# Fifteen small loads put ahead of the tail's loads on one issuing queue

## The chip, the core and the metric

The program runs on one core of one Trainium2 chip. The metric is the device time in microseconds (us) of that core. Data comes from the chip's memory through 16 DMA engines; the loads are issued by SyncE (SP), and one load of 128 rows is split over all 16 engines, 8 rows each. The engines that compute are TensorE (PE, with its weight loads as PEld), VectorE (DVE) and ScalarE (ACT); GpSimd (POOL) only builds constants at the start.

## What is computed

One token goes through attention with cached keys and values and then through a gated feed-forward layer, all in 32-bit floats. There are 32 heads with 8192 cached positions and 192 channels each, the model width is 640 and the hidden width 1536.

```
q      = (layernorm(x) @ wq) as 32 heads of 192
scores = q . k_cache * 192**-0.5            # 32 x 8192
o      = softmax(scores) . v_cache          # 32 x 192
h      = x + o @ wo
g, u   = layernorm(h) @ W_gate, layernorm(h) @ W_up
out    = h + (g * (g > 0) * u) @ W_down
```

Keys and values are 403 MB, and everything that is read is 446 MB. Each byte is used once.

## The kernel before, in words

The host lays the inputs out in rows of 128 partitions, one DRAM array for each load, so that a load is 128 long contiguous rows. Three big buffers on chip, slot_x, slot_y and slot_z, each hold up to 65,280 bytes in a partition. The loads go through them in turn: while one buffer is read by TensorE, the others are being filled.

The heads are worked through in this way. Head 0 is the start. Then a loop of 10 turns takes three heads in each turn (units a, b and c). A turn issues five loads: row_1 and row_2 of a turn at the end of the turn before, and row_3, row_4 and row_5 inside it. A unit multiplies the query with the keys (line 180), transposes the scores on DVE (line 385), takes the exponential on ACT (line 482) and multiplies with the values (line 187). The last head, the output projection and the feed-forward layer stand behind the loop, in a tail written out once.

What sets the order is a set of hand-written semaphores. SP waits until a buffer has been used up (free[i], counted by PE or DVE) and until its load before has landed (land[i]), then issues the next load into it. All loads stand in one SP program and are issued in the order of the code (line 533 is the helper that records every load). A load into slot_x in the tail, for example, stands behind a wait on free[4], which DVE gives once unit c of the last turn has used its keys.

Behind the loop's last turn SP issues, in this order: row_t1 into slot_x (keys of the last head and a quarter of the values of the head before), row_t2a and row_t2b into slot_z (values and projection weights), then, when free[5] has come, row_t3 and row_up into slot_y, then, when fin has come, row_gate and four pieces of row_down into slot_x. At the end, when the result stands in the tile o4 (fout), SP and ACT store one half of it each, and SP waits for both stores.

In the tail PE waits for row_t1 before the last head's scores (line 263), for row_t3 before the last values (line 280), for row_up before the up projection (line 300), for row_gate before the gate projection (line 306), and for the four pieces of row_down inside the down projection (lines 318 and 325). DVE multiplies up and gate (line 465) and transposes the product (line 466) between the last two.

Of the kernel before, what the change touches and what calls it, by code (L numbers as in the profile page):

```python
# [85 lines left out]
def build(nc, arrays):  # L86
    dram = {k: nc.dram_tensor(k, v.shape, F32, kind="ExternalInput").ap() for k, v in arrays.items()}
    out = nc.dram_tensor("out", (1, 1, D), F32, kind="ExternalOutput").ap()
    sb = lambda name, shape: nc.alloc_sbuf_tensor(name, list(shape), F32).ap()
# [26 lines left out]
    gu = sb("gu", [P, FG])  # L116
    guT = sb("guT", [P, FJ, 32])
    o4 = sb("o4", [P, DG])

    ps = lambda name, w: nc.alloc_psum_tensor(name, [P, w], F32).ap()  # L120
    sc = ps("sc", 1024)
# [2 lines left out]
    sem = nc.alloc_semaphore  # L124
# [3 lines left out]
    free = [sem(f"free{i}") for i in range(6)]  # L128
    tl = {n: sem(f"tl_{n}") for n in ("t1", "t2a", "t2b", "t3", "up", "gate", "d0", "d1", "d2", "d3")}
    fin, fout, hsem, out_a = (sem(n) for n in ("fin", "fout", "hsem", "out_a"))  # L130
    cst_pe, cst_ve, hdve, hrs, out_s = (sem(n) for n in ("cst_pe", "cst_ve", "hdve", "hrs", "out_s"))

    def wait(eng, s, n, sub=0, **kw):
        w = eng.wait_ge(s, n)  # L134
        if sub:
            w.then_inc(s, -sub)
        return w
# [392 lines left out]
    sp = nc.sync  # L530

    def load(t, src, s):
        sp.dma_start(t, src).then_inc(s, 16)

    def sync_program():
        load(Y[:, 0:W_P], dram["row_p"], land[5])
        r1, r2, r3, r4, r5 = (dram[f"row_{i}"] for i in range(1, 6))
        load(X[:, 0:W_1], r1[0], land[1])
        load(Z[:, 0:W_2], r2[0], land[2])

        def turn(i):
            wait(sp, free[5], 1, 1)
            wait(sp, land[5], 16, 16)
            load(Y[:, 0:W_3], r3[i], land[3])
            wait(sp, free[1], 2, 2)
            wait(sp, land[1], 16, 16)
            load(X[:, 0:W_4], r4[i], land[4])
            wait(sp, free[3], 2, 2)
            wait(sp, land[3], 16, 16)
            load(Y[:, 0:W_5], r5[i], land[5])  # L550
            wait(sp, free[2], 1, 1)
            wait(sp, land[2], 16, 16)
            wait(sp, free[4], 1, 1)
            wait(sp, land[4], 16, 16)

        with sp.Fori(0, NTURN - 1) as i:
            turn(i)
            load(X[:, 0:W_1], r1[i + 1], land[1])
            load(Z[:, 0:W_2], r2[i + 1], land[2])
        turn(NTURN - 1)  # L560
        load(X[:, 0:W_T1], dram["row_t1"], tl["t1"])
        load(Z[:, 0:W_T2A], dram["row_t2a"], tl["t2a"])
        load(Z[:, W_T2A:W_T2A + W_T2B], dram["row_t2b"], tl["t2b"])
        wait(sp, free[5], 1, 1)
        wait(sp, land[5], 16, 16)
        load(Y[:, 0:W_T3], dram["row_t3"], tl["t3"])
        load(Y[:, W_T3:W_T3 + W_UP], dram["row_up"], tl["up"])
        wait(sp, fin, 1, 1)
        load(X[:, 0:W_UP], dram["row_gate"], tl["gate"])
        for n, (a, b) in enumerate(DOWN):  # L570
            load(X[:, W_UP + a:W_UP + b], dram["row_down"][:, a:b], tl[f"d{n}"])
        wait(sp, fout, 1)
        load(out[0, 0, 0:D // 2].rearrange("(g n) -> g n", g=2), o4[31:33, :], out_s)
        wait(sp, out_s, 16, 16)
        wait(sp, out_a, 16, 16)
        wait(sp, fout, 1, 1)

    programs = ((ET.PE, tensor_program), (ET.DVE, vector_program), (ET.Activation, scalar_program),
                (ET.Pool, pool_program), (ET.SP, sync_program))
    for e, _ in programs:  # L580
        nc.br(f"prog_{e.name}", engines=[e])
# [13 lines left out]
```

## Time and profile before

| What | Value |
|---|---|
| median of 3 runs | 1038.7 us (1038.47 to 1038.83) |
| the profiled execution's own time | 1039.63 us |
| span in its profile | 1038.3 us |
| bytes read | 445.94 MB, 429 GB/s over the span |
| packets of the SP queue, share of the 16 DMA engines' time | 99.4% |
| PE busy | 547.4 us (53%) |
| DVE busy | 188.2 us (18%) |
| mean granted TensorE clock | 0.767 |

The span runs from the first to the last instruction that was recorded; 1.3 us of the profiled execution lie outside it. A DMA packet is what one engine moves for one row, and each load ends on each engine with a 4-byte packet that counts up the load's semaphore. In a narrow window the profile puts a packet's whole time at its start, so a DMA share above 1.00 there counts starts and not use. Instructions also come to the chip by DMA, in packets of 16 KB on a queue of their own ("q8 instruction").

### The profile page before, as it was taken

The numbers are of one execution on the slowest core, as the hardware profiler recorded it, in microseconds if no ns is written. First come the engines' busy times: TensorE is split into PE (matmuls) and PEld (weight loads), VectorE is DVE, ScalarE is ACT, GpSimd is POOL, SyncE is SP. The second block draws the span as 40 slices with busy tenths as digits, with TensorE's granted clock in tenths as the row PEclk, the third lists the DMA queues.
The fourth block names the chain that finished last, engine by engine and source line by source line (L and its number), as shares of the span: only waits on it lengthen the run. The fifth ranks groups of instructions, "written<-read, shape, count | busy, mean of one in ns | idle before, by whom it ended". The sixth has DMA issues, their size and how long they took to land. (4 is left out here: it accounts for less than half of the span.)

```text
span 1038.3 us, 10306 instructions
## 1 busy us (share of the span) xinstructions
PE 547.4 (53%) x4492; PEld 176.3 (17%) x4492; DVE 188.2 (18%) x478; ACT 41.2 (4%) x137; POOL 1.2 (0%) x11
## 2 busy tenths in 40 slices
PE   0746446456363563654544546536465463564676
PEld 0211112112121120111111112112111121121123
DVE  1211221112122021221121220212221121220111
ACT  1000000000000000000000000000000000000010
POOL 0000000000000000000000000000000000000000
PEclk9876867768677677776787867867877778687787
DMA  9999999999999999999999999999999999999997
GB/s 402 441 432 425 434 435 431 445 420 435 435 439 433 425 438 436 440 427 432 435 435 426 433 438 431 444 426 433 433 438 438 420 438 436 438 432 425 432 427 326
DMA packets 8800, 446.07 MB, mean 430 GB/s; under 512 B 980, under 2 KB 1112, under 8 KB 1240
## 3 DMA queue, kind: packets, MB, share of 16 engines
q1 hardware_dynamic: 8788, 445.94, 99.4%
q8 instruction: 7, 0.11, 0.0%
q14 instruction: 1, 0.01, 0.0%
q10 hardware_dynamic: 4, 0.00, 0.0%
HBM read 445.94 MB, written 0.00 MB: 429 GB/s over the span
## 5 line engine op out<-in xcount | busy, mean ns | idle before, releaser
L180 PE MATMUL sc<-slot_x,qs 128*32 128x512 f32 x1008 | 150.9, 743 | 109.6 <-DMA slot_x<-row 99.9
L187 PE MATMUL po<-slot_y,p 128*2 128x384 f32 x1152 | 117.9, 562 | 80.2 <-DMA slot_y<-row 77.4
L187 PE MATMUL po<-slot_z,p 128*2 128x384 f32 x560 | 72.5, 671 | 91.7 <-DMA slot_z<-row 88.4
L180 PE MATMUL sc<-slot_y,qs 128*32 128x512 f32 x288 | 54.1, 913 | 83.0 <-DMA slot_y<-row 82.5
L187 PE MATMUL po<-slot_x,p 128*2 128x384 f32 x336 | 43.6, 651 | 86.1 <-DMA slot_x<-row 86.1
L373 DVE COPY oc<-od 128x2 f32<-128x2 f32 x32 | 5.1, 159 | 389.5 <-PE od L206 389.5
L385 DVE STREAM_TRANSPOSE st<-sc 128x512 f32<-128x512 f32 x64 | 45.7, 714 | 164.4 <-PE sc L180 164.4
L180 PEld LDWEIGHTS sc<-slot_x,qs 128*32 128x32 f32 x1008 | 35.4, 134 | 200.8 <-DMA slot_x<-row 106.3
L187 PEld LDWEIGHTS po<-slot_y,p 128*2 128x2 f32 x1152 | 29.1, 94 | 167.7 <-DMA slot_y<-row 86.5
L391 DVE TENSOR_REDUCE m<-pt 128x1 f32<-128x128 f32 x32 | 9.3, 292 | 162.6 <-PE pt L199 162.6
L187 PEld LDWEIGHTS po<-slot_z,p 128*2 128x2 f32 x560 | 15.0, 102 | 138.3 <-DMA slot_z<-row 95.6
L474 ACT COPY qs<-q_ps 128x96 f32<-128x96 f32 x32 | 7.7, 239 | 766.9 <-ACTq L134 766.9
L367 DVE SCALAR_TENSOR_TENSOR prod<-slot_y,xn,prod 128x192 f32<-128x192 f32 x88 | 36.9, 419 | 3.1
L180 PEld LDWEIGHTS sc<-slot_y,qs 128*32 128x32 f32 x288 | 11.4, 154 | 113.8 <-DMA slot_y<-row 83.4
L180 PE MATMUL sc<-slot_z,qs 128*32 128x512 f32 x240 | 27.6, 592 | 0.0
L187 PEld LDWEIGHTS po<-slot_x,p 128*2 128x2 f32 x336 | 8.6, 94 | 109.5 <-DMA slot_x<-row 88.0
L203 PEld LDWEIGHTS od<-mrl,ob 128*128 128x128 f32 x132 | 18.1, 199 | 34.2 <-issue 34.2
L478 ACT COPY ob<-po 128x384 f32<-128x384 f32 x32 | 15.3, 479 | 181.1 <-ACTq L134 181.1
L203 PE MATMUL od<-mrl,ob 128*128 128x1 f32 x132 | 20.8, 262 | 1.6 <-PEq L134 1.6
L194 PE MATMUL q_ps<-pat,prod 128*128 128x96 f32 x64 | 15.4, 323 | 8.5 <-PEq L134 8.5
L365 DVE TENSOR_SCALAR prod<-slot_y,xn 128x192 f32<-128x192 f32 x22 | 6.9, 315 | 65.4 <-DMA slot_y<-row 65.3
L376 DVE SCALAR_TENSOR_TENSOR accs<-slot_y,oc,accs 128x640 f32<-128x640 f32 x21 | 18.5, 879 | 0.0
(95 smaller groups left out, 248.6 us busy)
## 6 DMA issues: line engine op xcount, KB each, us to landing
slot_x<-row SPq DMA_DIRECT2D x10, 8160.0 KB, 26.9
slot_z<-row SPq DMA_DIRECT2D x10, 8160.0 KB, 45.8
slot_y<-row SPq DMA_DIRECT2D x10, 8160.0 KB, 24.7
slot_x<-row SPq DMA_DIRECT2D x10, 7680.0 KB, 35.6
slot_y<-row SPq DMA_DIRECT2D x10, 7584.0 KB, 27.1
slot_x<-row_t SPq DMA_DIRECT2D x1, 7680.0 KB, 25.2
slot_y<-row_p SPq DMA_DIRECT2D x1, 7136.0 KB, 19.6
slot_z<-row_t2a SPq DMA_DIRECT2D x1, 5088.0 KB, 36.9
```

Source lines behind the costliest of these rows:

```text
L180: m = te.matmul(sc[Q(g), half * 512:half * 512 + 512], qs[:, 32 * part:32 * part + 32], blk(half, part * 4 + g), start=(part == 0), stop=( ...
L187: m = te.matmul(po[32 * g:32 * g + 2, 0:PW], p[:, 2 * i:2 * i + 2], blk(i), start=(i < 4), stop=(i >= 28))
L194: te.matmul(q_ps[:, 0:96], prod[:, 0:P], pat[:, 0, :], start=True, stop=False)
L203: te.matmul(od[:, 0:1], ob[:, k * DH:k * DH + P], mrl[:, k:k + 1], start=(k == 0), stop=(k == 1))
L365: dv(ve.tensor_scalar(prod, w3[:, 0, :], xn[:, 0:1], None, op0=ALU.mult), w=first)
L367: dv(STT(prod, w3[:, j, :], xn[:, j:j + 1], prod, op0=ALU.mult, op1=ALU.add), w="self", inc=d2p if j == DJ - 1 else None)
L373: dv(ve.tensor_copy(oc, od[:, 0:2]), w=pd())
L376: dv(STT(accs[:, 0:D], w[:, 0:D], oc[:, 0:1], accs[:, 0:D], op0=ALU.mult, op1=ALU.add), w="self", inc=inc)
L385: return dv(ve.transpose(st[:, s], sc[:, s]), w=w)
L391: dv(ve.reduce_max(vec["m1"], pt[:, 0:P], axis=AX.X, negate=True), w=pd(), inc=d2a)
L474: op(ac.copy(qs, q_ps[:, 0:96]), inc=a2p)
L478: op(ac.copy(ob, po[:, 0:PW]), inc=a2p)
```

## The change

A tile "mark" of 16 partitions and 2048 columns is added behind all other tiles, and a semaphore msem. Behind the loop's last turn and ahead of row_t1, SP issues fifteen loads into it: the first of 15 rows, the next of 14, down to one of 1 row, each row 128 floats (512 bytes) from the start of the first rows of row_up. Each goes to its own columns, nothing reads them, and nothing waits for them but one wait on msem (15 loads of 16 counts each) at the very end, between the wait for ACT's store and the last wait on fout. No other instruction is changed; lines behind the additions are numbered higher by 1, 2 and 4.

```diff
@@ tiles and semaphores
+    mark = sb("mark", [16, 2048])
...
+    msem = sem("msem")
@@ sync_program, behind the loop
         turn(NTURN - 1)
+        for k in range(15, 0, -1):
+            load(mark[0:k, 128 * k:128 * k + 128], dram["row_up"][0:k, 0:128], msem)
         load(X[:, 0:W_T1], dram["row_t1"], tl["t1"])
         load(Z[:, 0:W_T2A], dram["row_t2a"], tl["t2a"])
@@ sync_program, at its end
         wait(sp, out_s, 16, 16)
         wait(sp, out_a, 16, 16)
+        wait(sp, msem, 240, 240)
         wait(sp, fout, 1, 1)
```

On SP, behind the loop, this is the order before. The first row is the loop's last load into slot_y.

```order
L533 DMA slot_y<-row 128x15168
L533 DMA slot_x<-row_t 128x15360
L533 DMA slot_z<-row_t2a 128x10176
L533 DMA slot_z<-row_t2b 128x6144
L533 DMA slot_y<-row_t 128x7104
```

With the change, fifteen small loads stand between the first two of these rows. The last four of them and what follows read so:

```order
L535 DMA mark<-row_up 4x128
L535 DMA mark<-row_up 3x128
L535 DMA mark<-row_up 2x128
L535 DMA mark<-row_up 1x128
L535 DMA slot_x<-row_t 128x15360
L535 DMA slot_z<-row_t2a 128x10176
L535 DMA slot_z<-row_t2b 128x6144
```

The three loads row_t1, row_t2a and row_t2b, which SP issued at once when slot_x was free, are now issued behind fifteen others.

## The prediction, on record before the changed kernel ran

> **What bounds the kernel now.** I read the page first, then SP's own rows around the edit, then the packets of the DMA engines in narrow windows there, and last PE's rows at the end.
>
> ```profile
> span 1038.3 us, 10306 instructions
> ...
> DMA  9999999999999999999999999999999999999997
> ...
> q1 hardware_dynamic: 8788, 445.94, 99.4%
> ...
> 200.00:800.00 600.00, 314.77 (x2539) 98.17 (x2535) 107.78 (x268) 21.09 (x76) 0.00 (x0) 0.75 1.00 434
> ```
>
> The 16 DMA engines are busy for the whole span except its last slice, at 434 GB/s in the loop (last column). Whatever takes time away from them before that slice is lost, unless PE gives it back at the end. So the question is whether SP still issues row_t1 early enough.
>
> ```profile
> 932.94 0.33 SPq L533 DMA_DIRECT2D slot_y<-row  x1
> 953.58 0.33 SPq L533 DMA_DIRECT2D slot_x<-row_t  x1
> 953.96 0.43 SPq L533 DMA_DIRECT2D slot_z<-row_t2a  x1
> 954.43 0.43 SPq L533 DMA_DIRECT2D slot_z<-row_t2b  x1
> 989.76 0.33 SPq L533 DMA_DIRECT2D slot_y<-row_t  x1
> ...
> 990.69 0.35 SPq L533 DMA_DIRECT2D slot_x<-row_gate  x1
> 991.08 1.85 SPq L533 DMA_DIRECT2D slot_x<-row_down  x4
> 1036.88 0.34 SPq L533 DMA_DIRECT2D out<-o  x1
> ...
> 960.71 6.22 PE L187 MATMUL po<-slot_y,p 128*2 128x384 f32 x48 [7.38 <-DMA slot_y<-row]
> ```
>
> Columns: start, duration, engine, line, operation. The loop's last load goes out at 932.94 and PE has it at 960.71, its landing. SP waits until 953.58 for slot_x and then issues row_t1. At that moment the engines still have some 6.6 us of the loop's last load to move, and this is all the cover there is. How the 16 engines finish that load, by its 4-byte semaphore packets (the "under 512 B"), in the windows 958.1 to 958.9, 958.9 to 959.5, 959.5 to 959.8 and 959.8 to 960.3:
>
> ```profile
> DMA packets 20, 0.61 MB, mean 768 GB/s; under 512 B 10, under 2 KB 10, under 8 KB 10
> DMA packets 2, 0.06 MB, mean 102 GB/s; under 512 B 1, under 2 KB 1, under 8 KB 1
> DMA packets 4, 0.12 MB, mean 410 GB/s; under 512 B 2, under 2 KB 2, under 8 KB 2
> DMA packets 6, 0.18 MB, mean 369 GB/s; under 512 B 3, under 2 KB 3, under 8 KB 3
> ```
>
> Ten engines are done before 958.9, the last three between 959.8 and 960.3 (say 960.2; the landing is seen 0.5 us later). Each goes straight on with row_t1: packets come in pairs, a semaphore packet and a new row. Nobody waits for another engine, so the end belongs to the late ones.
>
> At the end, PE's rows:
>
> ```profile
> 1017.28 6.32 PE L300 MATMUL sc<-slot_y,hc 128*32 128x384 f32 x40
> 1026.02 5.13 PE L306 MATMUL sc<-slot_x,hc 128*32 128x384 f32 x40 [2.42 <-PEq L134]
> 1032.94 3.20 PE L318 MATMUL q_ps<-slot_x,guT 128*32 128x160 f32 x88 [1.79 <-PEq L134]
> 1036.47 0.38 DVE L467 SCALAR_TENSOR_TENSOR o<-q_ps,hr,h 128x160 f32<-128x160 f32 x1 [3.83 <-PE q_ps L325]
> ...
> slot_z<-row_t2b SPq DMA_DIRECT2D x1, 3072.0 KB, 43.7
> slot_x<-row_gate SPq DMA_DIRECT2D x1, 3840.0 KB, 35.2
> ...
> slot_x<-row_down SPq DMA_DIRECT2D x1, 160.0 KB, 42.6
> ```
>
> row_gate, issued at 990.69, lands 35.2 us later, at 1025.9, and PE's gate block starts at 1026.02. From there on a chain of compute runs to the end: gate 5.13 us, DVE's product and transpose, the down projection from 1032.94, the output. The last piece of row_down was issued at 991.08 + 3 x 0.47 = 992.5 and is there at 1035.1, over a microsecond before PE's last matmuls. So the end is the landing of row_gate plus 12.4 us.
>
> **The change, part by part.** First the **fifteen issues**. Back to back, SP starts a load every 0.47 us: row_t2a to row_t2b is 0.47, and the four pieces of row_down fill 1.85 us, (1.85 - 0.43) / 3 = 0.47, though they shrink from 1920 to 160 KB. Only the step from a load that was issued after a wait is 0.38. The fifteen loads take the places from 953.58 on, so row_t1 goes out at 953.58 + 0.38 + 14 x 0.47 = 960.5 (960.6 with unrounded steps) in place of 953.58. The bound from below: one load that stands alone takes 0.33 with 128 rows and 0.34 with the 2 rows of the store at 1036.88; with the 0.04 between two loads that is 0.37 each, and row_t1 would go out at 953.58 + 15 x 0.37 = 959.1. No row shows small loads in a row. I take 0.47, since the rows back to back are the nearest, and neither the size (four pieces) nor the number of rows (0.34 against 0.33) moves an issue in this trace.
>
> [...]
>
> Second, the **restart**. When row_t1 comes after the queue has run dry, the engines start from nothing, as they do at the kernel's start. Issue, then the packets in the windows 1.84 to 2.1 and 2.1 to 2.6 (none starts before), then the landing:
>
> ```profile
> 0.81 0.42 SPq L533 DMA_DIRECT2D slot_y<-row_p  x1
> DMA packets 13, 0.74 MB, mean 2854 GB/s; under 512 B 0, under 2 KB 0, under 8 KB 0
> DMA packets 3, 0.17 MB, mean 343 GB/s; under 512 B 0, under 2 KB 0, under 8 KB 0
> slot_y<-row_p SPq DMA_DIRECT2D x1, 7136.0 KB, 19.6
> ```
>
> The first data moves 1.0 us after the issue. 7136 KB are 7.31 MB, at 434 GB/s 16.8 us; the landing took 19.6, so 2.8 us are not transfer, and without the 0.5 us from the last packet to the landing, 2.3 us. That is my price from an issue to full rate; 1.0 is its lower bound. Row_t1 then streams as if from 960.6 + 2.3 = 962.9, where the latest engines of before began at 960.2: **+2.7 us**. The lower bounds would give 960.6 + 1.0 - 960.2 = 1.4. The upper: row_gate's last engine need not be one of the late three. Its semaphore packets, windows 1022.3 to 1024.5 and 1024.5 to 1026, and what else ran from 1020 to 1021.4:
>
> ```profile
> DMA packets 62, 0.84 MB, mean 384 GB/s; under 512 B 15, under 2 KB 15, under 8 KB 15
> DMA packets 42, 0.63 MB, mean 420 GB/s; under 512 B 1, under 2 KB 1, under 8 KB 1
> q8 instruction: 1, 0.02, 4.5%
> ```
>
> Fifteen engines are done by 1024.5, one later, behind an instruction packet of 16 x 1.4 us x 4.5% = 1.0 us. If that engine was one of the two that finished at about 959.7, it loses 3.2. I keep 2.7, with 1.4 and 3.2 as ends.
>
> Third, the **small packets**: 120 rows of 512 bytes, 61 KB, 0.14 us at 434 GB/s. Even if one engine got all fifteen of a kind, at 27 GB/s (434 / 16) and as much again for its semaphore packets it would lose under 1 us, behind the loop's last load and in the gap that is open anyway. I put it at 0; without the gap it would cost up to 0.8.
>
> Fourth, **one more wait at SP's end**. The 15 loads landed long ago, so it is one instruction: between 0.02 (the 17 ns of the row below) and 0.1, I take 0.05. It is passed while the stores return, or just behind them.
>
> ```profile
> L134 SPq EVENT_SEMAPHORE  x106: 17/17/17, 55.5 to 1038.3; - x106
> ```
>
> **What comes back.** Row_t2a, row_t2b, row_t3, row_up, row_gate and row_down follow row_t1 without a gap: row_t3 goes out at 989.76 and the engines have work until about 998 (row_t2b, 954.43 + 43.7), so that hangs on nothing new; all of it moves by the same 2.7. PE can give back some. The gate block ran 5.13 us at a mixed clock:
>
> ```profile
> 1015.00:1020.00 5.00, 3.77 (x24) 1.95 (x28) 2.11 (x10) 0.20 (x1) 0.00 (x0) 0.50 1.00 430
> 1025.00:1030.00 5.00, 3.98 (x29) 1.75 (x33) 0.00 (x0) 0.00 (x0) 0.00 (x0) 0.66 0.97 412
> 1030.00:1035.00 5.00, 3.21 (x77) 2.37 (x73) 1.40 (x2) 0.00 (x0) 0.00 (x0) 1.00 0.54 212
> ```
>
> The third number from the end of the line is the granted clock: 0.50 under the up block (6.32 us for the same 40 matmuls), 0.66 and then 1.00 under the gate block. At 1.00 throughout it would take about half of 6.32, 3.2 us. So a changed clock is worth from -1.9 to +1.2 us, and the gain is cut at about -1.2, since the last row_down, moved too, then ends the chain (1036.4 - 1035.1). I take -0.4: the idle 2.42 us ahead of the gate may shrink.
>
> Sum, on the profiled span: 2.7 + 0 + 0.05 - 0.4 = 2.35, 1038.3 to 1040.65. The profiled execution (1039.63) lies 0.9 over the median; on the median, 1038.7 + 2.35 = **1041.0 us**.
>
> **The rivals.** *Small loads are issued faster* (0.37): row_t1 at 959.1, stream from 961.4, 1.2 late; 1.2 + 0.05 - 0.4 gives 1039.6. For it: the load that stands alone. Against it: every row back to back.
>
> *All hidden*: row_t1 must be out 2.3 before 960.2, so an issue may take (957.9 - 953.58) / 15 = 0.29. No load here is under 0.33. Time 1038.75.
>
> *SP is held up*: before, at most eight loads were under way (from row_t2b to the last row_down, at 992.5). If the queue took no more, SP would stop behind the loop's last load and seven small ones until 960.7, then issue eight more: row_t1 at 960.7 + 8 x 0.47 = 964.5, stream from 966.8, 6.6 late, 1045.0. Nothing shows such a limit, nothing excludes it.
>
> *Faster*: the tail's compute moves relative to the clock, the gate block runs at 1.00 and gains 1.2; it decides if the loads come less than 1.2 late, by the two first rivals. With the hidden one, 1037.6; with the faster issue, no change.
>
> **How the numbers follow.** Forecast 0.55, faster issue 0.25, hidden 0.07, held up 0.08, faster 0.05. A measurement of this kernel tells 0.2%, 2.1 us, from no change; slower begins at 1040.8. The forecast's own range is 1039.7 (restart 1.0, and all else as it is) to 1042.2 (3.2 late, and the clock worse by 0.3), and about 0.40 of its 0.55 lies over 1040.8; with the held-up case and a little of the faster issue, slower has 0.50. Faster has 0.05, the rest, 0.45, is the same. The range 1039.1 to 1042.6 takes in the faster issue and leaves out the hidden, the held-up and the faster case.
>
> **What would show it.** In the new trace: fifteen rows at 0.47 us and row_t1 at about 960.6 (959.1 is the first rival, over 961 the third); a DMA share under 1 between 960 and 963; the landing of row_gate at about 1028.6 in place of 1025.9; PE's gate block between 3.2 and 6.3 us. I am wrong if row_t1 is issued before 958, or if it is late and row_gate is not, or if the end moves without them.

## The result and the profile after

| | before | with the change |
|---|---|---|
| median of 18 runs each, run in turn | 1038.81 us | 1040.38 us |
| lowest and highest | 1038.07 to 1040.87 | 1039.31 to 1042.36 |
| ratio, 95% interval | | 1.0014 (1.0007 to 1.002) |
| profiled execution, its span | 1039.63, 1038.3 | 1040.78, 1039.4 |

The change costs 1.57 us, with an interval of 0.7 to 2.1 us. The forecast was 2.3 us on the median (1038.7 to 1041.0). One run of a later experiment (behind_pad, 1067.09 us at a granted clock of 0.545, where its other runs have 0.752 to 0.767) was in a slow state and is left out of its medians.

SP's rows of the changed kernel around the edit and at the end (start, duration, engine, line, operation):

```profile
933.56 0.33 SPq L535 DMA_DIRECT2D slot_y<-row  x1
952.50 5.31 SPq L535 DMA_DIRECT2D mark<-row_up  x15
957.86 0.36 SPq L535 DMA_DIRECT2D slot_x<-row_t  x1
958.25 0.43 SPq L535 DMA_DIRECT2D slot_z<-row_t2a  x1
...
991.82 0.36 SPq L535 DMA_DIRECT2D slot_x<-row_gate  x1
992.23 1.91 SPq L535 DMA_DIRECT2D slot_x<-row_down  x4
1037.58 0.27 SPq L535 DMA_DIRECT2D out<-o  x1
```

The fifteen issues take 5.36 us, from 952.50 to 957.86, and not 7.0. That is 0.357 us from one start to the next, less than the lower bound of the prediction (0.37). In this execution slot_x came free 1.08 us earlier than in the profile of before, while the loop's last load landed at the same time (PE starts on it at 960.90, before at 960.71), so the lateness is best counted from the time at which slot_x is free. It also means that the cover was longer here: the last engine was done with that load at about 960.4 (0.5 us before PE starts on it), 7.9 us after slot_x was free, where the profile of before had 6.6.

What one small load takes, in nanoseconds (shortest, median, longest of the fifteen):

```profile
L535 SPq DMA_DIRECT2D mark<-row_up x15: 252/297/408, 952.5 to 957.6; - x15
```

The packets on the page of before and then of the changed kernel:

```profile
DMA packets 8800, 446.07 MB, mean 430 GB/s; under 512 B 980, under 2 KB 1112, under 8 KB 1240
```

```profile
DMA packets 9040, 446.13 MB, mean 429 GB/s; under 512 B 1100, under 2 KB 1352, under 8 KB 1480
```

There are 240 more packets: 120 rows of 512 bytes, and 120 semaphore packets (those under 512 bytes). A load ends with one semaphore packet on each engine that it uses (before, 16 for each of the 61 loads of 128 rows and 4 for the stores make the 980), and 15 + 14 + ... + 1 = 120: so a load of k rows used k engines here.

The DMA engines in the same 30 us of the two kernels, and in the 3 us for which the prediction named a share under 1, before first (last two columns: share of their time, GB/s):

```profile
955.00:985.00 30.00, 14.64 (x117) 4.75 (x121) 4.13 (x12) 1.11 (x4) 0.00 (x0) 0.72 0.99 428
960.00:963.00 3.00, 2.29 (x16) 0.55 (x20) 2.17 (x6) 0.00 (x0) 0.00 (x0) 0.50 1.04 451
```

```profile
955.00:985.00 30.00, 14.17 (x102) 4.17 (x103) 3.54 (x8) 1.11 (x4) 0.00 (x0) 0.66 0.98 412
960.00:963.00 3.00, 2.10 (x16) 0.55 (x20) 1.98 (x6) 0.00 (x0) 0.00 (x0) 0.50 0.84 351
```

Over the 30 us 16 GB/s are missing; divided by 434 GB/s that is 1.1 us of full rate. The share is almost the same (0.98 for 0.99): the engines hardly stand idle, they move less while they are busy. (The 3 us count packets that start there, so their 0.84 isn't idle time either.) The first row of row_t1 on each of the 16 engines, with the packets just ahead of it, shows where the time goes: windows 958.1 to 960.25 before and 958.3 to 960.6 with the change.

```profile
DMA packets 32, 0.98 MB, mean 457 GB/s; under 512 B 16, under 2 KB 16, under 8 KB 16
q1 hardware_dynamic: 32, 0.98, 106.0%
```

```profile
DMA packets 272, 1.05 MB, mean 454 GB/s; under 512 B 136, under 2 KB 256, under 8 KB 256
q1 hardware_dynamic: 272, 1.05, 144.9%
```

Each window holds 16 rows of row_t1, the second also the 120 small rows; the rest are semaphore packets. 106.0% of 2.15 us are 2.28 us for each engine, 144.9% of 2.3 us are 3.33 us, 1.05 us more on the mean. Read packet by packet in the trace, a small row with its semaphore packet takes 0.03 us, 0.22 us for a mean engine. The larger part is the first row of row_t1 itself: 2.27 or 2.28 us on every engine before, 2.65 to 3.97 us on 13 of the 16 with the change.

The transfers' times from issue to landing (last column), of the changed kernel:

```profile
slot_x<-row_t SPq DMA_DIRECT2D x1, 7680.0 KB, 22.0
...
slot_x<-row_gate SPq DMA_DIRECT2D x1, 3840.0 KB, 34.8
...
slot_x<-row_down SPq DMA_DIRECT2D x1, 160.0 KB, 42.1
```

With the issue times above, row_t1 lands at 979.9, row_gate at 1026.6 and the last row_down (issued at 992.23 + 1.91 - 0.43 = 993.7) at 1035.8. In the profile of before it was 978.8 (953.58 and 25.2 us), 1025.9 and 1035.1. So all of the tail is 0.7 to 1.1 us late in these two executions; as that of before is 0.8 us over the median of its 18 runs and that of the change 0.4 us, the typical distance is larger. PE follows, with the same durations as before:

```profile
1026.72 5.13 PE L308 MATMUL sc<-slot_x,hc 128*32 128x384 f32 x40 [3.63 <-PEq L136]
1033.64 3.20 PE L320 MATMUL q_ps<-slot_x,guT 128*32 128x160 f32 x88 [1.79 <-PEq L136]
1037.16 0.38 DVE L469 SCALAR_TENSOR_TENSOR o<-q_ps,hr,h 128x160 f32<-128x160 f32 x1 [3.83 <-PE q_ps L327]
```

The gate block starts 0.70 us later than before, and DVE's last row 0.69. A second, smaller part comes after all computing: SP's waits at its very end, in two windows of the changed kernel, 1038.6 to 1038.95 and 1039.25 to 1039.6 (none starts between them).

```profile
L136 SPq EVENT_SEMAPHORE  x2: 17/17/17, 1038.7 to 1038.9; - x2
...
L136 SPq EVENT_SEMAPHORE  x2: 17/17/17, 1039.3 to 1039.4; - x2
```

The two waits for the stores are passed at 1038.7 and 1038.9; the new wait, whose loads landed some 80 us earlier, is passed only at 1039.3, 0.45 us later. In the profile of before three waits lie between 1038.0 and 1038.3 in a row. The prediction had 0.05 us for this.

So three things may have a share: row_t1 is issued late, there are more packets (and a slower row behind them), and SP stops for 0.45 us. The experiments take them one at a time.

### The profile page after: what moved, and what is told of

Same layout as the page of the kernel before. It is cut to its first block, busy times and chain, and to the rows that moved or that the text cites. A ratio compares the mean times of both kernels' runs of the same rounds, so it can differ in the third digit from the quotient of the medians.

```text
span 1039.4 us, 10322 instructions
## 1 busy us (share of the span) xinstructions
PE 547.2 (53%) x4492; PEld 175.4 (17%) x4492; DVE 188.2 (18%) x478; ACT 41.2 (4%) x137; POOL 1.2 (0%) x11
## 5 line engine op out<-in xcount | busy, mean ns | idle before, releaser
L182 PE MATMUL sc<-slot_x,qs 128*32 128x512 f32 x1008 | 147.5, 728 | 104.2 <-DMA slot_x<-row 94.1
L189 PE MATMUL po<-slot_y,p 128*2 128x384 f32 x1152 | 125.1, 590 | 82.7 <-DMA slot_y<-row 79.8
L189 PE MATMUL po<-slot_z,p 128*2 128x384 f32 x560 | 70.3, 653 | 93.8 <-DMA slot_z<-row 90.6
```

Of the source, the lines that this page charges most:

```text
L182: m = te.matmul(sc[Q(g), half * 512:half * 512 + 512], qs[:, 32 * part:32 * part + 32], blk(half, part * 4 + g), start=(part == 0), stop=( ...
L189: m = te.matmul(po[32 * g:32 * g + 2, 0:PW], p[:, 2 * i:2 * i + 2], blk(i), start=(i < 4), stop=(i >= 28))
```

## The experiments

In all of them the small loads go to places that nothing reads and the semaphore counts only count, so every output is computed as before; the count in the last wait on msem follows them and is not always shown. Each kernel ran 11 times, thirty 5 times and pace once. Where a time is set against the kernel before, the runs were taken in turn on one chip; intervals are of 95%. The span is the median over a kernel's runs; the median span of before was 1037.0 or 1037.1 in each of these comparisons, so I take 1037.05.

| label | time, us | against before | ratio | median span | against 1037.05 |
|---|---|---|---|---|---|
| (the change) | 1040.38 | +1.57 | 1.0014 (1.0007 to 1.002) | 1038.9 | +1.85 |
| delay | 1039.81 | +1.27 | 1.0009 (0.9999 to 1.0018) | 1038.0 | +0.95 |
| eight | 1039.62 | +1.08 | 1.0012 (1.0003 to 1.0022) | 1037.9 | +0.85 |
| behind | 1040.14 | +1.60 | 1.0018 (1.0009 to 1.0027) | 1038.5 | +1.45 |
| thirty | 1045.34 | +6.80 | 1.0066 (1.0052 to 1.008) | 1043.9 | +6.85 |
| gate2 | 1038.71 | -0.04 | 1.0003 (0.9994 to 1.0012) | 1037.0 | -0.05 |
| gate2_marks | 1040.37 | +1.62 | 1.0016 (1.0007 to 1.0025) | 1038.7 | +1.65 |
| pad | 1038.86 | +0.09 | 1.0004 (0.9995 to 1.0013) | 1037.5 | +0.45 |
| after_pad | 1040.27 | +1.50 | 1.0012 (1.0003 to 1.0021) | 1038.5 | +1.45 |
| behind_pad | 1039.51 | +0.74 | 1.0004 (0.9995 to 1.0013) | 1037.95 | +0.9 |
| sixteen_pad | 1040.78 | +2.01 | 1.0018 (1.0009 to 1.0027) | 1039.4 | +2.35 |
| ones_pad | 1038.92 | +0.22 | 1.0001 (0.9992 to 1.001) | 1037.5 | +0.45 |

An interval is about 1 us to each side, so no two neighbours of this table are told apart by their times alone. The reading below rests on the spans and on the rows of the profiles as well, and says where that is not enough. A span is not the time either: what lies outside it is 1.3 to 1.4 us in some runs of every kernel and 1.6 to 2.0 us in the others, and how many are of which kind differs from kernel to kernel.

### Late issue or packets: delay, behind, eight, thirty

**delay** makes SP just as late without moving a byte: 75 counts of the semaphore in place of the loads.

```diff
-        for k in range(15, 0, -1):
-            load(mark[0:k, 128 * k:128 * k + 128], dram["row_up"][0:k, 0:128], msem)
+        for k in range(75):
+            sp.sem_inc(msem, 1)
         load(X[:, 0:W_T1], dram["row_t1"], tl["t1"])
```

> No small load at all; in their place SP runs 75 semaphore counts, about 0.07 us each, so that row_t1 goes out some 5.3 us after slot_x is free. Late issue: as slow as the change, +1.6 us against before (1.0 to 2.2). Small packets: 0.

**behind** keeps the loads, and lets row_t1 go first (against the kernel before).

```diff
         load(X[:, 0:W_T1], dram["row_t1"], tl["t1"])
         load(Z[:, 0:W_T2A], dram["row_t2a"], tl["t2a"])
         load(Z[:, W_T2A:W_T2A + W_T2B], dram["row_t2b"], tl["t2b"])
+        for k in range(15, 0, -1):
+            load(mark[0:k, 128 * k:128 * k + 128], dram["row_up"][0:k, 0:128], msem)
```

> The same fifteen small loads, issued behind row_t2b instead of ahead of row_t1. Late issue (what costs is that row_t1 goes out 5.4 us later): row_t1 goes out when slot_x is free, the same bytes move, and the time is that of before, within 0.3 us. Small packets (the 120 packets and their semaphore counts cost DMA time or upset the balance of the 16 engines): the 1.6 us of the change stay. The tail's clock (the 1.6 us are a shifted clock gate at the end): undecided, 0 to 1.6.

SP's row_t1 in the profile of delay and how long row_t1 and row_gate took from issue to landing there:

```profile
957.62 0.33 SPq L535 DMA_DIRECT2D slot_x<-row_t  x1
```

```profile
slot_x<-row_t SPq DMA_DIRECT2D x1, 7680.0 KB, 22.2
```

Row_t1 goes out at 957.62 (957.86 with the change) and lands at 979.8, as with the change. The span is 0.95 us longer; the time, 1.27 us longer, isn't clear of its interval. So lateness alone, without one packet more, delays row_t1 as the change does. But behind, where row_t1 goes out at 952.57, is no faster than the change within the intervals (part of its +1.45 is the same stop at the end: two of its last waits are passed at 1038.6 and 1038.8, the others from 1039.25 on). Late issue alone, which I had held for the whole cause, cannot be it: the packets cost something too, or the loads cost something elsewhere.

**eight** keeps the first eight of the fifteen loads, of 15 rows down to 8.

```diff
-        for k in range(15, 0, -1):
+        for k in range(15, 7, -1):
             load(mark[0:k, 128 * k:128 * k + 128], dram["row_up"][0:k, 0:128], msem)
```

> Only the first eight of the fifteen loads (15 rows down to 8; 92 of the 120 packets), ahead of row_t1, which then goes out 2.9 us late, about 3 us before most engines run dry. Late issue: covered, 0 to +0.4 us. Small packets: 92/120 of the change, +1.2 us. A queue that takes at most eight loads: as the change or more.

The eight took 3.06 us, so row_t1 went out 3.1 us late, well inside the cover of 6.6 us less the 2.3 us that the prediction gives to a restart. The span is still 0.85 us longer. Eight loads of 15 to 8 rows are 92 of the 120 rows; that too speaks for a share of the packets. The window 958.1 to 960.45, again with the 16 first rows of row_t1, bears it out:

```profile
DMA packets 216, 1.03 MB, mean 439 GB/s; under 512 B 108, under 2 KB 200, under 8 KB 200
q1 hardware_dynamic: 216, 1.03, 128.2%
```

128.2% of 2.35 us are 3.01 us for each engine, 0.73 more than before. Packet by packet, the 92 small rows take 0.17 us of a mean engine, and 13 first rows of row_t1 take 2.41 to 3.24 us in place of 2.27. No engine ran dry: the cover held, and still there was a price.

**thirty** issues all of them twice, into rows 0 to 15 and 16 to 31 of a larger tile.

```diff
-    mark = sb("mark", [16, 2048])
+    mark = sb("mark", [32, 2048])
...
-        for k in range(15, 0, -1):
-            load(mark[0:k, 128 * k:128 * k + 128], dram["row_up"][0:k, 0:128], msem)
+        for r in (0, 16):
+            for k in range(15, 0, -1):
+                load(mark[r:r + k, 128 * k:128 * k + 128], dram["row_up"][0:k, 0:128], msem)
```

> The fifteen loads twice (the second set on other partitions of a tile of 32), ahead of row_t1, which goes out some 10.7 us late. Late issue: all engines are dry by then, so that each further microsecond of issue counts in full: 5.4 more than the change, +6.5 to +7.3 us against before. Small packets: twice the change, +3.2 us. A queue limit would show as a pause in SP's row.

SP's rows, and the DMA engines around row_t1's issue:

```profile
953.35 10.64 SPq L535 DMA_DIRECT2D mark<-row_up  x30
964.03 0.36 SPq L535 DMA_DIRECT2D slot_x<-row_t  x1
964.81 0.35 SPq L535 DMA_DIRECT2D slot_z<-row_t2a  x1
```

```profile
963.00:964.00 1.00, 1.00 (x12) 0.29 (x8) 0.89 (x2) 0.00 (x0) 0.00 (x0) 0.50 0.03 8
964.00:965.00 1.00, 1.00 (x12) 0.22 (x8) 0.00 (x0) 0.00 (x0) 0.00 (x0) 0.55 0.01 3
965.00:966.00 1.00, 1.00 (x20) 0.31 (x16) 0.00 (x0) 0.00 (x0) 0.00 (x0) 1.00 3.02 983
```

```profile
slot_x<-row_t SPq DMA_DIRECT2D x1, 7680.0 KB, 21.2
```

Here the queue is dry and the price of a restart can be read by itself: nothing but small packets moves until 965, 1.0 us after the issue. 7680 KB are 7.864 MB, 18.1 us at 434 GB/s; the landing took 21.2, less 0.5 us from the last packet to the landing leaves 2.6 us from issue to full rate (the prediction had 2.3). Row_t1 is 10.68 us late here, and 10.68 + 2.6 - 6.6 of cover = 6.7 us; measured were 6.85 in the span and 6.8 in the time. So beyond the cover the lateness counts in full here, and the prediction's sum holds. The 16 first rows of row_t1 take 3.02 us on the mean here, so some 0.75 us of the restart is the slower first row.

### How long an issue takes: pace

In place of the fifteen loads, five each of 1, 2, 8, 15, 16, 32, 64 and 128 rows (32 floats a row) into a larger tile behind row_t2b; a single profiled run, 1043.77 us.

```diff
+        for n, k in enumerate((1, 2, 8, 15, 16, 32, 64, 128)):
+            for i in range(5):
+                c = 32 * (5 * n + i)
+                load(mark[0:k, c:c + 32], dram["row_up"][0:k, 0:32], msem)
```

> A probe of the issue's pace, behind row_t2b, where SP waits anyway: five loads each of 1, 2, 8, 15, 16, 32, 64 and 128 rows, each row 32 floats. The prediction took 0.47 us from start to start whatever the rows; the change ran at 0.36. Pace by rows: 0.36 up to some number of rows, then growing to 0.47 at 128. Pace by engines used: a step between 15 and 16 rows and none from 16 to 128. Pace by something else (a source with long rows): 0.36 at 128 rows too.

SP's small loads in the windows of the groups, in order: 1, 2, 8 and 15 rows, the first two of 16 rows, then a window with the second of 16 once more, the other three of 16, the five of 32 and the first of 64, then the other four of 64, and those of 128 (nanoseconds: shortest, median, longest; a group's first still shows the group ahead of it):

```profile
L535 SPq DMA_DIRECT2D mark<-row_up x5: 238/252/337, 953.8 to 955.0; - x5
...
L535 SPq DMA_DIRECT2D mark<-row_up x5: 250/253/254, 955.3 to 956.5; - x5
...
L535 SPq DMA_DIRECT2D mark<-row_up x5: 272/295/295, 956.8 to 958.1; - x5
...
L535 SPq DMA_DIRECT2D mark<-row_up x5: 323/402/403, 958.5 to 960.2; - x5
...
L535 SPq DMA_DIRECT2D mark<-row_up x2: 387/403/419, 960.6 to 961.1; - x2
...
L535 SPq DMA_DIRECT2D mark<-row_up x10: 419/3391/4488, 961.1 to 989.2; - x10
...
L535 SPq DMA_DIRECT2D mark<-row_up x4: 596/597/1787, 992.0 to 995.1; - x4
...
L535 SPq DMA_DIRECT2D mark<-row_up x5: 432/432/586, 995.7 to 997.8; - x5
```

An issue has no fixed price: 0.25 us for 1 or 2 rows, 0.295 for 8, 0.40 for 15, 0.60 for 64 and 0.43 for 128. And from the third load of 16 rows on, SP is held up: up to 4.49 us for one load. Each load of 16 rows gives one row and one semaphore packet to each engine, and one row of row_t1 takes 2.27 us on an engine (61440 bytes at 27 GB/s), so 4.49 us are about two of the rows ahead. That would fit a queue which is full and takes the next load's two packets when two older ones are done; the trace does not show the queue itself. I count some 72 packets in it at that point on an engine that has a row of every small load (what is left of three big loads of 9 packets each, and two for each of 22 or 23 small loads), an estimate from this trace. SP being held up, as in the prediction's third rival, is thus measured, but not at eight loads: here 22 small ones went out unhindered, and in the change none of the fifteen took more than 0.41 us.

### Does the clock under the gate hide something: gate2, gate2_marks

The prediction let the whole end hang on row_gate. **gate2** is the kernel before with row_gate in two loads, so that four fifths of the gate block can start earlier; **gate2_marks** is the same edit on the change.

```diff
-        load(X[:, 0:W_UP], dram["row_gate"], tl["gate"])
+        load(X[:, 0:4 * F], dram["row_gate"][:, 0:4 * F], tl["gate"])
+        load(X[:, 4 * F:W_UP], dram["row_gate"][:, 4 * F:W_UP], tl["gate2"])
...
         for j in range(DJ):
+            if j == DJ - 1:
+                wait(te, tl["gate2"], 16, 16)
             for g in range(4):
```

> The kernel before, with row_gate in two loads (its first four fifths, then the last fifth) on two semaphores, so that PE starts the gate block when the first has landed. The prediction says that the end is the landing of row_gate plus 12.4 us, and that row_down's last piece ends the chain about 1.2 us earlier. If so, 0.9 to 1.3 us faster than before (1037.6). If PE's end does not hang on row_gate, no change.

> The changed kernel with row_gate in the same two loads: the end then hangs on the DMA engines alone. Late issue: +1.0 us (the delay of the last engine in the profile of the change, 1.0 at row_t1 and 0.7 at row_gate) against the two-part kernel without the small loads, so about as fast as before, -0.4 to +0.4 us. If the 1.6 us of the change are the clock at the end, as fast as the two-part kernel without small loads, -1.1 us.

PE's rows at the end of gate2, and the landing of the last row_down there:

```profile
1023.85 3.43 PE L308 MATMUL sc<-slot_x,hc 128*32 128x384 f32 x40 [1.25 <-PEq L134]
1030.17 2.66 PE L320 MATMUL q_ps<-slot_x,guT 128*32 128x160 f32 x48 [2.90 <-PEq L134]
1033.29 2.10 PE L320 MATMUL q_ps<-slot_x,guT 128*32 128x160 f32 x40 [0.45 <-PEq L134]
```

```profile
slot_x<-row_down SPq DMA_DIRECT2D x1, 160.0 KB, 41.1
```

The gate block is done 3.9 us earlier than in the profile of before (1027.28 for 1031.15), and nothing is won: 1038.71 for 1038.75, where 0.9 to 1.3 us had been expected. The down projection now breaks in two and waits for a landing of row_down. The profile of pad (below), whose gate block was not split, has the same break behind a gate block of 3.43 us:

```profile
1024.93 3.43 PE L308 MATMUL sc<-slot_x,hc 128*32 128x384 f32 x40 [2.38 <-PEq L136]
1030.16 1.84 PE L320 MATMUL q_ps<-slot_x,guT 128*32 128x160 f32 x48 [1.79 <-PEq L136]
1032.65 1.62 PE L320 MATMUL q_ps<-slot_x,guT 128*32 128x160 f32 x40 [0.66 <-PEq L136]
```

So the profile of before, with 5.13 us under the gate and 0.9 us over the median, showed one way in which an execution ends, and in others the last row_down's landing ends it (in pad it lands at 1034.0, and PE's last part starts at 1034.06). The change costs about the same on both: 1.66 us from gate2 to gate2_marks (1040.37 against 1038.71), 1.57 on the kernel before, each to about 1 us. That gate2_marks would be as fast as the kernel before was a miss. The cost is thus no matter of PE's clock at the end.

### SP's stop at its end: pad, after_pad

**pad** is the kernel before with fifteen semaphore counts behind row_t2b, where SP idles, and the wait at the end. No load is added.

```diff
         load(Z[:, W_T2A:W_T2A + W_T2B], dram["row_t2b"], tl["t2b"])
+        for k in range(15):
+            sp.sem_inc(msem, 1)
...
         wait(sp, out_a, 16, 16)
+        wait(sp, msem, 15, 15)
         wait(sp, fout, 1, 1)
```

> No small load; fifteen semaphore counts behind row_t2b, where SP waits anyway, and the wait on msem at the end: SP's program is as long as that of the change, and nothing else differs from before. Program length (the sixteenth added instruction lies where SP stops 0.4 us to get on in its program): a gap of 0.45 us ahead of the wait on msem in SP's rows, and a span 0.4 to 0.5 us longer than before's (37.1 to 37.5 over 1000). Loads alone: no gap, 0 to 0.1 us.

**after_pad** is the change with twenty counts behind row_t2b, which moves every later instruction of SP down by twenty places.

```diff
         load(Z[:, W_T2A:W_T2A + W_T2B], dram["row_t2b"], tl["t2b"])
+        for k in range(20):
+            sp.sem_inc(msem, 1)
...
-        wait(sp, msem, 240, 240)
+        wait(sp, msem, 260, 260)
```

> The changed kernel with twenty semaphore counts more behind row_t2b, so that the place where SP stops comes while it waits for slot_y anyway. Program length: no gap at the end, 0.4 us less than the change (span 1038.5 in place of 1038.9, +1.5 against before's spans). If the stop is none of the program's length: as the change.

SP's last waits in pad (1036.2 to 1036.5 and 1036.89 to 1037.1, none between), then in after_pad (1030 to 1042):

```profile
L136 SPq EVENT_SEMAPHORE  x2: 17/17/17, 1036.3 to 1036.4; - x2
...
L136 SPq EVENT_SEMAPHORE  x2: 17/17/17, 1036.9 to 1037.0; - x2
```

```profile
L136 SPq EVENT_SEMAPHORE  x4: 17/17/17, 1038.8 to 1039.1; - x4
```

The 0.45 us are in pad without any load, and gone in after_pad with all of them. In thirty the same pause stands between row_t1 and row_t2a: 964.03 + 0.36 to 964.81, 0.42 us, where two loads in a row are else 0.04 apart. So in these kernels SP pauses at a fixed place of its program, and fifteen more instructions put its very last waits behind that place. Counted in the traces it is the same place each time, ahead of SP's 296th recorded instruction: in the change, gate2_marks, behind, pad, after_pad, the three other kernels with twenty counts, delay, thirty and pace. Before has only 281, and eight 290, and neither shows the pause.

In the spans it is 0.45 (pad) and 0.4 (the change against after_pad). The times do not show it: pad is 0.09 us slower than before, with an interval of -0.5 to +1.3 us, and the change stands 1.57 us above before, after_pad 1.50. In 9 of 11 runs of pad the part outside the span is the shorter kind, and in a good half of the runs of before the longer, so what the span gains may in part be lost outside it. That the pause costs time is not shown.

Why SP pauses there isn't shown. One row goes with it: in each of these kernels an instruction packet of 8 KB on the queue q14 starts 0.6 to 5.8 us behind the pause (thirty at 970.6, after_pad at 965.3), and before has none there. Whether that packet has to do with the pause is not shown either; the pause was 0.42 to 0.45 us in the open wherever SP had something to do.

### What the packets cost: behind_pad, sixteen_pad, ones_pad

Behind row_t2b, and followed by the twenty counts so that the pause falls where SP idles, stand the fifteen loads as they are (**behind_pad**), all with 16 rows (**sixteen_pad**), or all with one (**ones_pad**); the diff is against the kernel before.

```diff
         load(Z[:, W_T2A:W_T2A + W_T2B], dram["row_t2b"], tl["t2b"])
+        for k in range(15, 0, -1):
+            load(mark[0:k, 128 * k:128 * k + 128], dram["row_up"][0:k, 0:128], msem)
+        for k in range(20):
+            sp.sem_inc(msem, 1)
```

The other two have 0:16 or 0:1 in place of 0:k, of mark and of row_up.

> The small loads behind row_t2b and the twenty counts behind them: neither a late row_t1 nor a stop at the end is left. Small packets (120 rows and their semaphore counts, and a slower first row behind them, cost the DMA engines 0.6 to 1.1 us): span +0.6 to +1.1 against before. Late issue and program length alone: 0.

> As the last kernel, but all fifteen small loads have 16 rows, one for each engine: 240 small packets in place of 120, fifteen on every engine in place of fifteen on one and none on another. If the slowest engine's packets cost (15 x 0.036 = 0.54 us and a slower first row, 0.3): +0.8 to +1.1 us on every engine, at least what the staircase costs. If the total counts: twice the staircase.

> As the kernel with fifteen loads of 16 rows, but each load has one row: if a load of k rows uses the first k engines, all fifteen packets fall on one engine and the others get nothing. Then that engine loses 0.5 to 0.9 us and the rest nothing, and since the engines finish up to 2 us apart and another one is mostly the last, the span grows by 0 to 0.4 us. If a load costs all engines, whatever its rows: as the staircase.

The spans are +0.9, +2.35 and +0.45 us for 120, 240 and 15 rows. The three grow with the rows, and only that of 240 rows stands clear of no change in the times (2.0 us, 0.9 to 2.8). In ones_pad the fifteen rows start one after another, 0.03 us apart (996.21 to 996.63), as on a single engine; in sixteen_pad every engine gets fifteen. The most loaded engine has the same work in both, and the spans are 1.9 us apart. The packets, read one by one, show why.

How much later the 16 engines end row_t1 and row_t3, on the mean and counted from their ends of the loop's last load, against before, pad and gate2 (which agree to 0.01 us for row_t1 and to 0.08 for row_t3), all in us, one profiled execution each:

| label | end of row_t1 | end of row_t3 | small packets | slower rows | median span |
|---|---|---|---|---|---|
| eight | +0.67 | +0.49 | 0.17 | 0.49 | +0.85 |
| delay | +0.92 | +0.89 | 0 | 0.60 | +0.95 |
| (the change) | +1.11 | +0.96 | 0.22 | 0.75 | +1.85 |
| after_pad | +1.50 | +1.34 | 0.22 | 0.50 | +1.45 |
| thirty | +7.14 | +6.99 | 0.45 | 0.76 | +6.85 |
| behind_pad | +0.04 | +0.79 | 0.22 | 0.57 | +0.9 |
| sixteen_pad | +0.04 | +2.28 | 0.45 | 1.53 | +2.35 |
| ones_pad | +0.05 | +0.24 | 0.03 | 0.09 | +0.45 |

In the last three kernels the rows behind the small packets are those of row_t3. They take 1.06 us on the mean before; in sixteen_pad the first ones on the engines mostly take 1.94 to 2.33 us and many second ones 1.4 to 1.7, and in ones_pad one row takes 2.09. So the cost goes with the small packets that an engine has itself, and is mostly slower rows behind them: 1.53 us on the mean in sixteen_pad, 0.09 in ones_pad. (The profile of sixteen_pad is of an execution 2.8 us over its median, 1043.57 us; it was already late ahead of the small loads.) In the upper part what the two columns leave of the end of row_t1 is idle time: none in eight, 0.14 in the change, 0.32 in delay, 0.78 in after_pad, 5.93 in thirty. Row_t1's first rows are slow in delay too, where no small packet stands ahead of them: 0.60 us on the mean with a late issue alone.

SP's second to fourth row_down in behind (nanoseconds; the longest is the third):

```profile
L535 SPq DMA_DIRECT2D slot_x<-row_down x3: 430/431/1517, 992.3 to 994.3; - x3
```

With small packets behind row_t2b SP is also held up at row_down (1.52 us for 0.43; 4.23 in sixteen_pad, 1.70 in ones_pad). In the change, where the small packets are moved by then, the four pieces take 1.91 as before (1.85). The place behind row_t2b thus isn't the change with its lateness taken away: it has a cost of its own.

## Why the prediction was right, point by point

The time, 1040.38, was in the range (1039.1 to 1042.6), 0.6 us under the forecast of 1041.0; 1.57 us is less than the 0.2% (2.1 us) that were set as the bound of slower. That it would be slower by more than these 2.1 us had been given 0.50, that it would stay within them 0.45; it stayed within them. The number is right in part by luck: two terms were mis-sized in opposite directions, and the lateness came about in another way than the sum has it.

1. **The fifteen issues: mis-sized.** The step that neither the size nor the number of rows "moves an issue in this trace" took 0.47 from start to start. Measured were 0.357 on the mean; the load itself took between 0.25 and 0.41 by its rows. Row_t1 was 5.36 us late and not 7.0. The step leaned on rows that all have 128 partitions; the one row with 2 stood alone. By the prediction's own sum the measured lateness gives 5.36 + 2.3 - 6.6 = +1.0 in place of 2.7. Row_t1 landed 1.1 later, row_gate 0.7, delay's span is 0.95 longer. But the 6.6 us of cover are those of one execution. In the change's own the cover was 7.9: row_t1 went out at 957.86, 957.86 + 2.3 = 960.2, and the last engine was done at 960.4, so the sum gives nothing, and row_t1 landed late all the same. The prediction had named a row_t1 ahead of 958 as a sign of being wrong. That sign was there: 1.08 us of it are the earlier slot_x, and 1.64 the faster issues. The first rival's pace (0.37) was the nearer one, though its time of 1039.6 was not nearer. The 0.43 us that a load behind another takes before the change are those of 128 rows (0.43 in pace too); for 1 to 16 rows the traces have 0.25 to 0.42. In pace the first load of 15 rows, behind one of 8, took 0.32 us, and the next 0.40.

2. **The restart: right in size for a dry queue, but not what the change paid.** 1.0 us to the first data and 2.3 to full rate were predicted; thirty shows 1.0 and 2.6. In the change the engines stand idle for only 0.14 us on the mean; what costs is that 13 of 16 first rows of row_t1 are slower, 0.75 us on the mean. One of the late engines is among them: its first row starts at 960.11 and takes 3.42 us. So "Each goes straight on with row_t1" and "the end belongs to the late ones" hold for when an engine starts, and miss how long its first row takes. Eight shows the same with the cover intact.

3. **The small packets, put at 0: too low.** Behind row_t2b they cost 0.9 in the span (behind_pad), about the 0.8 named for packets without a gap. In the change their own time is 0.22 us on a mean engine. How much of the slower rows is theirs and how much the late issue's can't be told, as delay has slow rows without them. After_pad, without SP's pause, has +1.45, and delay +0.95; the difference, 0.5, is smaller than the intervals.

4. **The wait at SP's end: mis-sized.** 0.05 us (at most 0.1) were predicted for the span; 0.45 came. In the time it isn't shown (pad +0.09). The row of 17 ns was right for a wait, but the step didn't ask what the added instructions do to SP's program. It isn't the wait that lengthens the span, but the pause, as pad and after_pad show.

5. **What PE gives back, -0.4: not there.** The gate block took 5.13 us in both profiles, and gate2 shows that a faster one wins nothing. The step "the end is the landing of row_gate plus 12.4 us" held for the profiled executions of before and of the change; pad's ended on the last row_down.

By the packets of the change's own profile, 0.75 of slower rows, 0.22 of small packets and 0.14 of idle time are 1.1 us; with the pause of 0.45 that is 1.55 in the span, where the medians are 1.85 apart and the times 1.57.

The held-up rival fell with its number of eight loads, though SP was held up in pace, by up to 4.49 us for one load. The hidden one fell too, though row_t1 was out at 957.86 and its condition was 957.9: row_t1 was late at its landing. The faster one did not occur.

**What stays open:** why a row behind small packets, or behind a late issue, takes longer, and so how the 0.75 us divide between the two; what SP waits for in its pause; and whether the pause costs any time.

## What to carry to other kernels

Price an added load by rows of its own shape, and bound it from below well under the lone row that looks like it: in pace the issue took from 0.25 to 0.60 us by the number of rows alone. When a stream is kept fed by a queue, compare the lateness plus the restart with the cover, and take the cover from more than one execution (here 6.6 to 7.9 us); what was left over counted in full in thirty (6.7 us by the sum, 6.8 in the time). Lateness within the cover was not free here either: eight cost 0.85 us of span with no engine idle. Added instructions that moved nothing also lengthened the span here (pad, 0.45 us), since they shift all that follows in SP's program: a copy with as many idle instructions and no work tells that apart.

## What the runs showed of the hardware that was not expected

- The issue of a load was not monotone in its rows: 0.40 us for 15, 0.60 for 64, 0.43 for 128 (pace).
- From the third load of 16 rows on SP was held up, by up to 4.49 us for one load (pace), with some 72 packets waiting on an engine by an estimate from that trace; a row_down that stands 38 us behind the small loads was still held up by 1.1 us (behind).
- A large row behind small packets took longer than the same row without them: 1.94 to 2.33 us in place of 1.06 in sixteen_pad, and, with a late issue besides, up to 3.24 us in place of 2.27 in eight, where no engine had run dry.
- SP paused for 0.42 to 0.45 us ahead of the 296th instruction that the trace records of it, wherever that falls (pad, thirty, delay, after_pad).
- 240 rows of 512 bytes, 123 KB or 0.28 us at 434 GB/s, cost 2.35 us of span while the engines are busy (sixteen_pad): some eight times their bytes.
- The profiled execution of before was 0.9 us over the median and ended in another way than pad's or gate2's.
